# Moving the key and query transposes of a fused attention and double-FFN kernel: where they are issued, when their split copies run, and two small edits beside them

## The chip, the core and the metric

The kernel runs on one core of a Trainium2 chip. The metric is the device time of one execution in microseconds (us), the lower the better. One execution before the change was recorded by the hardware profiler; its trace is what all rows below are read from. The engines are named as the profile names them: PE (TensorE, the matrix engine; PEld is its weight load), DVE (VectorE), ACT (ScalarE), POOL (GpSimd), SP (SyncE, which here issues DMAs).

## The reference

What is computed is a local-and-global attention over 2 batches, 8 heads, 768 positions and 64 dimensions a head, and two dense feed-forward layers (FFN) on its result:

```python
# attention: 8 global keys, a causal window of 96 keys
scores = scale * q @ k.T + bias          # bias = -slope[h] * distance
scores = where(is_global | is_local, scores, -1e9)
a = exp(scores - scores.max(-1)); a = a / (a.sum(-1) + 1e-9)
x = (a @ v) rearranged to (1536 tokens, 512)
# FFN 1
h = x @ w_in1;  g = max(h, 0) + log1p(exp(-|h|));  x = g @ w_out1
# FFN 2
h = x @ w_in2;  g = h / (1 + exp(-1.702 * h));     out = g @ w_out2
```

All inputs and outputs are fp32. w_in has shape 512 x 2048 and w_out 2048 x 512 in both layers.

## The kernel before

Every product that needs fp32 precision is made of three matmuls on a high and a low part of each operand (`kh`, `kl`, `qh`, `ql` for keys and queries, `gh`, `gl` in the FFN). ACT makes the high part as a rounding copy, and DVE makes the low part as the difference to it; so `kl` always comes after its `kh`, and `ql` after its `qh`.

The attention runs over 12 blocks n of 128 queries. Each block has two halves g of four heads, which gives 24 halves s = 2n + g. One trip of the loop `for s in range(ns + 3)` issues work of several halves, in the order in which it is written (the scheduler is switched off there, and every engine takes its instructions in that order):

- on PE: `turn_r` (L540, tile `qps`, the reciprocal sums spread over a tile, odd trips only), `turn(s-1)` (L608, tile `t`, transposes of the exponentials), `scores(s+1)` (L571, tiles `s`), `turn_q` or `turn_k` (both through `turned`, L489, tile `qps`: four transposes of a block's queries or keys), `values(s-2)` (L630, tile `o`);
- on ACT: `split_q` (L504, `qh`) or `split_k` (L516, `kh`), `weights_of(s)` (L596, four exponentials with their sums, tile `pr`), in odd trips one operation of the weight converter that `tick` releases (L145, tile `t`, or L155, tile `w`) and `copy_r` (L545, `y`), then `copy_p(s-1)` (L615, or L617 for a narrow half, tile `pt`), which brings the transposed exponentials from PSUM to SBUF;
- on DVE: pieces of the weight converter (L143 to L160), the low part `ql` (L506) or `kl` (L518), `reduce(s+1)` (L584: bias added, minimum taken, tiles `pr` and `mins`), and in even trips `weigh` (L531, L532) and `normalise` (L553 to L555, tiles `y`, `x0h`, `x0l`).

"Even" and "odd" below mean the parity of s in its trip. Three buffers matter. The PSUM tile `t` of `turn` exists once (`ps_t`, one buffer of two banks), so that `turn(s)` can't begin before `copy_p(s-1)` has read it. The `qps` tiles alternate between the PSUM banks `h2` and `h3` of `h_pool`, in the order in which they are asked for; `turn_k`, `turn_r` and `turn_q` share them. The first FFN unit, `first(0)` (L254, tile `h`), takes `h2` too, and is issued in trips 20 to 22. A block that begins a batch has 128 keys only, one that doesn't has 256, called narrow and wide here.

`check_counts` (L95 to L99) does five tiny DVE operations on the two scalars n_global and n_local. At the end of the kernel `staged` copies the last four accumulators of FFN 2 from PSUM to SBUF, one for each 128 rows of the result; the last of them is cut in two column halves, the first copied by DVE (L322) and the second by ACT (L323). `drain` sends each of the four out by one DMA (L365), the last from ACT's queue.

Of the kernel before, what the change touches and what calls it, by code (L numbers as in the profile page):

```python
# [8 lines left out]
F32 = mybir.dt.float32  # L9
# [4 lines left out]
AF = mybir.ActivationFunctionType  # L14
# [3 lines left out]
P = 128  # L18
# [7 lines left out]
TB = 512  # L26
# [9 lines left out]
def attention_two_ffns(ctx: ExitStack, tc: tile.TileContext, q, k, v, n_global, n_local,  # L36
# [10 lines left out]
    nc = tc.nc  # L47
# [16 lines left out]
    conv = ctx.enter_context(tc.tile_pool(name="conv", bufs=3))  # L64
# [29 lines left out]
    def check_counts():  # L94
        nc.vector.tensor_scalar(flag[:, 0:1], NL, 1.0, None, op0=ALU.is_lt)  # L95
        nc.vector.tensor_scalar(flag[:, 1:2], NL, float(WIN), None, op0=ALU.is_gt)
        nc.vector.tensor_tensor(flag[:, 0:1], flag[:, 0:1], flag[:, 1:2], op=ALU.max)
        nc.vector.tensor_scalar(flag[:, 1:2], NG, float(GLB), None, op0=ALU.is_gt)
        nc.vector.tensor_tensor(flag[:, 0:1], flag[:, 0:1], flag[:, 1:2], op=ALU.max)  # L99
# [128 lines left out]
    def ffn_phase(x1, slots, work, h_pool, weights, converter):  # L228
# [8 lines left out]
        acc, gs, st, part, pools = {}, {}, {}, {}, {}  # L237
# [77 lines left out]
        def staged(t, l, last=False):  # L315

            for m in range(4):
                if m % 2 == 0:
                    both = conv.tile([P, 2, TB], F32, tag="t", name="o")
                o = both[:, m % 2, :]  # L320
                if last and m == 3:
                    nc.vector.tensor_copy(o[:, :TB // 2], acc[l, t][m][:, :TB // 2])  # L322
                    nc.scalar.activation(o[:, TB // 2:], acc[l, t][m][:, TB // 2:], AF.Copy)  # L323
                elif m % 2:
                    nc.vector.tensor_copy(o, acc[l, t][m])
                else:
                    nc.scalar.activation(o, acc[l, t][m], AF.Copy)  # L327
                yield m, o, both
# [20 lines left out]
        def drain(l, t):  # L349
            if l == 0:  # L350
                xh, xl = x_tiles(f"y{t}")
                xs[1, t] = (xh, xl)
                sums = acc[l, t]
                if t in part:
                    sums = part[t]
                    for m in range(4):
                        nc.vector.tensor_tensor(sums[m], sums[m], acc[l, t][m], op=ALU.add)
                for m in range(4):
                    nc.scalar.activation(xh[:, m, :], sums[m], AF.Copy)
                    e = nc.gpsimd if t in part else nc.vector  # L360
                    e.tensor_tensor(xl[:, m, :], sums[m], xh[:, m, :].bitcast(F32), op=ALU.subtract)
            else:
                for m, o, _ in staged(t, 1, t == 0):
                    q = nc.scalar if t == 0 and m == 3 else nc.sync
                    q.dma_start(out[t * TB + m * P:t * TB + (m + 1) * P, :], o)  # L365

        def rest(u0, parts, acc_pool):
            pools.update(parts=parts, acc=acc_pool)
# [22 lines left out]
    def split_attention(actx, x1, h_pool, converter, first, bend, budget=1600):  # L391
# [100 lines left out]
        def own(i):  # L492

            return WIN + GLB + i % RING * BLK


        def turn_q(n):
            qts[n] = turned(raw[n]["qn"], n == 1)
# [10 lines left out]
        def turn_k(n):  # L509
            raw[n]["kn"] = turned(raw[n]["kn"], n == 1)  # L510
# [49 lines left out]
        def scores(s):  # L560
            n, g = halves[s]
            i = blocks[n][1]
            w, at = (NW, own(i) - WIN - GLB) if i else (P, own(0))
            qh, ql = qts[n]
            banks = [h_pool.tile([P, TB], F32, tag=f"h{e}", name=f"s{e}") for e in range(2)]
            ps[s] = ([x.rearrange("p (j k) -> p j k", j=2) for x in banks], w)
            for j in range(2):
                for m, (a, c) in enumerate(((qh, kh), (qh, kl), (ql, kh))):
                    for e in range(2):
                        es = slice(e * D, (e + 1) * D)  # L570
                        nc.tensor.matmul(ps[s][0][e][:, j, :w], lhsT=a[es, 2 * g + j, :],  # L571
                                         rhs=c[es, 2 * g + j, at:at + w], start=m == 0, stop=m == 2)

        def reduce(s):

            n, g = halves[s]
            banks, w = ps.pop(s)
            pr = pr_pool.tile([P, 2, 2, NW], F32, tag="pr", name="pr")
            table = bias_w if w == NW else bias_0
            prs[s] = (pr, w)  # L580
            for j in range(2):
                for e in range(2):
                    h = 4 * g + 2 * j + e
                    nc.vector.tensor_tensor_reduce(pr[:, j, e, :w], banks[e][:, j, :w], table[:, h, :], 1.0, 3.0e38,  # L584
                                                   op0=ALU.add, op1=ALU.min,
                                                   accum_out=mins[:, H * n + h:H * n + h + 1])
# [13 lines left out]
        def turn(s):  # L600
            pr, w = prs[s]
            nch = w // P
            t = ps_t.tile([P, 2 * TB], F32, tag="t", name="t")
            t = t.rearrange("p (j c e k) -> p j c e k", j=2, c=2, e=2)
            for j in range(2):
                for c in range(nch):
                    for e in range(2):
                        nc.tensor.transpose(t[:, j, c, e, :], pr[:, j, e, c * P:(c + 1) * P], ident)  # L608
            pts[s] = (t, nch)

        def copy_p(s):
            t, nch = pts[s]
            pt = p_pool.tile([P, 2, 2, 2, P], F32, tag="pt", name="pt")
            if nch == 2:
                nc.scalar.activation(pt, t, AF.Copy)  # L615
            else:
                nc.scalar.activation(pt[:, :, 0], t[:, :, 0], AF.Copy)  # L617
            pts[s] = pt
            prs.pop(s)
# [13 lines left out]
        def run(*parts):  # L633
            for part in parts:
                for _ in part or ():
                    pass

        ns = len(halves)
        nb = len(blocks)
# [21 lines left out]
        load(3)  # L661
        yield
        scores(0)
        reduce(0)
        turn_q(1)
        for s in range(ns + 3):
            n, g = divmod(s, 2)
            live = n < nb
            if g == 1 and 0 < n < nb - 3:
                load(n + 3)  # L670
            if g == 0 and 0 < n < nb:
                load_v(n)

            if g == 1 and 0 <= n - 1 < nb:
                turn_r(n - 1)
            if s >= 1 and s - 1 < ns:
                turn(s - 1)
            if s + 1 < ns:
                scores(s + 1)
            if s == 0:  # L680
                spin(5)
            if s == 1:
                turn_q(2)

            kept = iter(())
            if g == 0 and n + 1 < nb:
                kept = split_k(n + 1)
            if g == 1 and 1 < n + 1 < nb - 1:
                kept = split_q(n + 2)
            if s != 2:  # L690
                next(kept, None)
            if live:
                weights_of(s)
            if s == 1:
                copy_p(0)
            converter.tick()
            if s == 0:
                window_masks()
                bias(bias_w, dw, 0)
            if g == 0 and 0 <= n - 1 < nb:  # L700
                weigh(n - 1)
            if s > 1 and g == 0:
                converter.pump(budget // 2)
            run(kept)
            if s > 1 and g == 1:
                converter.pump(budget // 2)
            if s + 1 < ns:
                reduce(s + 1)
            if s == 0:
                bias(bias_w, dw, 4)  # L710
            if s < 2:
                run(split_q(s + 1))
            if s == 4:
                check_counts()
            if g == 0 and 0 <= n - 2 < nb:
                normalise(n - 2)
            if s > 1:
                converter.pump(budget // 2 * (s == 2 or g) if s + 1 < ns else budget)
            if g == 1 and 0 <= n - 1 < nb:
                copy_r(n - 1)  # L720
            if 1 < s <= ns:
                copy_p(s - 1)
            if g == 0 and 0 < n < nb - 2:
                turn_q(n + 2)
            if g == 1 and n + 2 < nb:
                turn_k(n + 2)
            if s >= 2 and s - 2 < ns:
                values(s - 2)

            if ns - 4 <= s < ns - 1:  # L730
                first(0, ((0,), (1,), (2, 3))[s - ns + 4])
            if ns - 1 <= s < ns + 2:
                bend(s - ns + 1)
                if s < ns + 1:
                    first(s - ns + 2)
            yield
# [173 lines left out]
```

## Time and profile before

| quantity | value |
|---|---|
| median of 3 runs | 642.05 us (641.81 to 642.26) |
| the profiled execution, its own time | 641.64 us |
| its span in the trace | 639.8 us |
| granted TensorE clock, mean | 0.999 of full speed |
| PE busy | 624.7 us (98%) |
| DVE busy | 397.5 us (62%) |
| ACT busy | 368.9 us (58%) |
| POOL busy | 20.6 us (3%) |
| chain that ended last | PE 90%, DVE 7%, DMA 1%, issue 1% |

The span is what the trace shows from its first instruction to its last; the execution's own time lies 1.8 us above it. Busy shares are means over the whole span, in which the attention (to about 118 us, mixed with the first FFN units from about 95 us) and the FFN (to about 633 us) differ much from each other.

### The profile page before, as it was taken

Reading aid. Unit: us, or ns where it says so; the run is one execution under the profiler, and the core shown is the slowest. Engines: PE = TensorE matmul, PEld = TensorE weight load, DVE = VectorE, ACT = ScalarE, POOL = GpSimd, SP = SyncE. Lnnn points to the kernel's source line nnn. Section 1 sums busy time; section 2 is a strip of 40 time slices with the busy share of each in tenths; the row PEclk is TensorE's granted clock in tenths of the full one; section 3 lists DMA queues with packets and bytes.
Section 4 is the critical chain, followed back from the end, with each engine's and each line's share of the span. In section 5 each row is a group of like instructions: output and inputs, shape, how many; then the busy total and the mean of one; then the engine's idle time right before and its main releaser. Section 6 shows DMA issues by size and latency. Waiting matters only on the chain.

```text
span 639.8 us, 9005 instructions
## 1 busy us (share of the span) xinstructions
PE 624.7 (98%) x3443; PEld 515.0 (80%) x3443; DVE 397.5 (62%) x757; ACT 368.9 (58%) x683; POOL 20.6 (3%) x46
## 2 busy tenths in 40 slices
PE   8899999999999999999999999999999999999995
PEld 7687778887888888888888888888888888888884
DVE  6999999799999757999469996751121111211111
ACT  6999998778787667887567863532232222222221
POOL 3200100000000000000000022000000000000000
PEclk9999999999999999999999999999999999999999
DMA  9967846931000003520015670000010000100001
GB/s 213 255 165 168 191 135 218 345 127 59 8 2 0 1 0 132 197 67 1 0 66 188 211 237 24 0 1 1 0 67 0 2 0 1 66 1 1 0 1 71
DMA packets 65715, 51.52 MB, mean 81 GB/s; under 512 B 41920, under 2 KB 58304, under 8 KB 65664
## 3 DMA queue, kind: packets, MB, share of 16 engines
q1 hardware_dynamic: 65232, 50.60, 27.1%
q8 instruction: 29, 0.48, 0.3%
q10 hardware_dynamic: 432, 0.26, 0.1%
q14 instruction: 22, 0.18, 0.1%
HBM read 44.70 MB, written 4.19 MB: 76 GB/s over the span
## 4 chain that ended last, share of the span: by engine, by line
PE 90%; DVE 7%; DMA 1%; issue 1%; SPq 0%; POOL 0%; ACT 0%; DVEq 0%; POOLq 0%
PE h L254 41%; PE acc L306 21%; PE acc L308 20%; DVE pr L584 2%; PE o L630 2%; PE t L608 2%; PE s L571 1%; PE qps L540 1%; PE qps L489 1%; DMA raw<-in_moe_w_out 1%; PE spin L419 1%; DVE t L153 1%; DVE kl L518 1%; DVE y L553 0%; DVE ql L506 0%
## 5 line engine op out<-in xcount | busy, mean ns | idle before, releaser
L275 DVE TENSOR_TENSOR gl<-g,gh 128x512 fp32r<-128x512 f32 x96 | 67.2, 700 | 173.4 <-ACT gh L273 173.2
L306 PE MATMUL acc<-gh,w 128*128 128x512 f32 x384 | 126.4, 390 | 0.0
L308 PE MATMUL acc<-w,gh 128*128 128x512 f32 x384 | 125.6, 389 | 0.0
L273 ACT ACTIVATE gh<-g 128x512 fp32r<-128x512 f32 x96 | 60.4, 629 | 88.3 <-PE acc L308 81.5
L306 PEld LDWEIGHTS acc<-gh,w 128*128 128x128 f32 x384 | 72.1, 188 | 15.2 <-ACT o L327 0.4
L308 PEld LDWEIGHTS acc<-w,gh 128*128 128x128 f32 x384 | 72.1, 188 | 15.1
L281 ACT ACTIVATE g<-h 128x512 f32<-128x512 f32 x48 | 28.7, 598 | 91.8 <-PE h L254 85.5
L306 PE MATMUL acc<-gl,w 128*128 128x512 f32 x192 | 75.1, 391 | 0.0
L308 PE MATMUL acc<-w,gl 128*128 128x512 f32 x192 | 74.7, 389 | 0.0
L284 ACT ACTIVATE e<-h 128x512 f32<-128x512 f32 x48 | 28.5, 593 | 39.4 <-PE h L254 37.1
L262 DVE SCALAR_TENSOR_TENSOR g<-c,g 128x512 f32<-128x512 f32 x48 | 32.9, 686 | 25.2 <-ACT g L288 25.1
L596 ACT ACTIVATE pr<-pr,mins 128x256 f32<-128x256 f32 (+1 forms) x96 | 45.8, 483 | 2.4 <-DVE mins L584 2.2
L254 PE MATMUL h<-x0h,w 128*128 128x512 f32 x128 | 43.2, 396 | 0.1
L306 PEld LDWEIGHTS acc<-gl,w 128*128 128x128 f32 x192 | 36.0, 188 | 8.7 <-DVE gl L275 1.3
L155 ACT ACTIVATE w<-t 128x1024 fp32r<-128x1024 f32 x32 | 33.8, 1058 | 15.1 <-DVE t L153 12.2
L254 PE MATMUL h<-y0h,w 128*128 128x512 f32 x128 | 42.0, 389 | 0.0
L254 PE MATMUL h<-y2h,w 128*128 128x512 f32 x128 | 42.0, 389 | 0.0
L254 PE MATMUL h<-x1h,w 128*128 128x512 f32 x128 | 42.0, 389 | 0.0
L254 PE MATMUL h<-y1h,w 128*128 128x512 f32 x128 | 42.0, 389 | 0.0
L254 PE MATMUL h<-x2h,w 128*128 128x512 f32 x128 | 42.0, 389 | 0.0
L308 PEld LDWEIGHTS acc<-w,gl 128*128 128x128 f32 x192 | 36.0, 188 | 7.4
L153 DVE SCALAR_TENSOR_TENSOR t<-raw,t 128x1024 int32<-128x1024 int32 x32 | 39.9, 1247 | 2.3 <-ACT t L145 2.3
(134 smaller groups left out, 1128.8 us busy)
## 6 DMA issues: line engine op xcount, KB each, us to landing
raw<-in_moe_w_in SPq DMA_DIRECT2D x32, 512.0 KB, 4.6
raw<-in_moe_w_out SPq DMA_DIRECT2D x32, 512.0 KB, 5.6
kn<-in_k SPq DMA_DIRECT2D x12, 256.0 KB, 4.4
qn<-in_q SPq DMA_DIRECT2D x12, 256.0 KB, 4.9
vn<-in_v SPq DMA_DIRECT2D x12, 256.0 KB, 3.5
out<-o SPq DMA_DIRECT2D x11, 256.0 KB, 2.1
vp<-vn SPq DMA_DIRECT2D x10, 192.0 KB, 3.9
part<-o SPq DMA_DIRECT2D x2, 512.0 KB, 3.8
```

The costliest lines, as they stand in the source:

```text
L153: nc.vector.scalar_tensor_tensor(t, top, -2 ** 31, t, op0=ALU.bitwise_and, op1=ALU.bitwise_or)
L155: s["later"](lambda: nc.scalar.activation(w[:, 0, :], t.bitcast(F32), AF.Copy))
L254: nc.tensor.matmul(h, lhsT=w[:, a, c * P:(c + 1) * P], rhs=b[:, c, :], start=c == 0 and n == 0, stop=c == KD - 1 and n == 2)
L262: nc.vector.scalar_tensor_tensor(st[u - 1]["g"], st[u - 1]["c"], -1.0, st[u - 1]["g"], op0=ALU.add, op1=ALU.subtract)
L273: nc.scalar.activation(gh, g, AF.Copy)
L275: nc.vector.tensor_tensor(gl, g, gh.bitcast(F32), op=ALU.subtract)
L281: nc.scalar.activation(g, s["h"], AF.Gelu_apprx_sigmoid)
L284: nc.scalar.activation(e, s["h"], AF.Abs)
L306: nc.tensor.matmul(o, lhsT=wo[:, a, ms], rhs=g, **kw)
L308: nc.tensor.matmul(o, lhsT=g[:, ms], rhs=wo[:, a, :], **kw)
L584: nc.vector.tensor_tensor_reduce(pr[:, j, e, :w], banks[e][:, j, :w], table[:, h, :], 1.0, 3.0e38, op0=ALU.add, op1=ALU.min, accum_out=min ...
L596: nc.scalar.activation(pr[:, j, e, :w], pr[:, j, e, :w], AF.Exp, bias=mins[:, H * n + h:H * n + h + 1], scale=-1.0, accum_out=sums[n][:, h ...
```

## The change

It has four parts.

1. `turn_k` and `turn_q` move from the end of a trip to right behind `turn(s-1)` of a later trip, ahead of `scores(s+1)`. `turn_k(n+1)` is now issued in the even trip of block n (before: at the end of the odd trip ahead of it), and `turn_q(n+2)` in the odd trip of block n (before: in the even trip ahead of it).
2. The split is cut in two places of a trip: the high part (`kh`, `qh`, ACT) now stands behind the exponentials of `weights_of(s)`, and the low part (`kl`, `ql`, DVE) behind the minima of `reduce(s+1)`. Before, both stood ahead of these.
3. `check_counts` moves from trip 4 to ahead of `reduce(0)`, before the loop.
4. The last 128 rows, which DVE and ACT copy in halves, get a buffer for each half, and go out by two DMAs of half the columns (one from SP, one from ACT) in place of one from ACT.

```diff
                 if last and m == 3:
+                    other = conv.tile([P, TB], F32, tag="t", name="o")
                     nc.vector.tensor_copy(o[:, :TB // 2], acc[l, t][m][:, :TB // 2])
-                    nc.scalar.activation(o[:, TB // 2:], acc[l, t][m][:, TB // 2:], AF.Copy)
+                    nc.scalar.activation(other[:, TB // 2:], acc[l, t][m][:, TB // 2:], AF.Copy)
+                    o = o, other
...
-                    q = nc.scalar if t == 0 and m == 3 else nc.sync
-                    q.dma_start(out[t * TB + m * P:t * TB + (m + 1) * P, :], o)
+                    rows = slice(t * TB + m * P, t * TB + (m + 1) * P)
+                    if isinstance(o, tuple):
+                        for q, part_of, c in zip((nc.sync, nc.scalar), o, (slice(0, TB // 2), slice(TB // 2, TB))):
+                            q.dma_start(out[rows, c], part_of[:, c])
+                    else:
+                        nc.sync.dma_start(out[rows, :], o)
...
         scores(0)
+        check_counts()
         reduce(0)
...
                 turn(s - 1)
+            if g == 0 and 2 <= n + 1 < nb:
+                turn_k(n + 1)
+            if g == 1 and 3 <= n + 2 < nb:
+                turn_q(n + 2)
             if s + 1 < ns:
                 scores(s + 1)
...
-            if g == 1 and 1 < n + 1 < nb - 1:
+            if g == 1 and 3 <= n + 2 < nb:
                 kept = split_q(n + 2)
-            if s != 2:
-                next(kept, None)
+            if s == 0:
+                next(kept)
             if live:
                 weights_of(s)
             if s == 1:
                 copy_p(0)
+            if s > 0:
+                next(kept, None)
             converter.tick()
...
-            run(kept)
+            if s == 0:
+                run(kept)
             if s > 1 and g == 1:
                 converter.pump(budget // 2)
             if s + 1 < ns:
                 reduce(s + 1)
+            run(kept)
...
-            if s == 4:
-                check_counts()
...
-            if g == 0 and 0 < n < nb - 2:
-                turn_q(n + 2)
-            if g == 1 and n + 2 < nb:
-                turn_k(n + 2)
```

In the changed file every line from `staged`'s new tile on stands 2 to 6 lines further down: L489 becomes L495, L504 L510, L540 L546, L571 L577, L584 L590, L608 L614, L615 L621, L630 L636.

PE's order, two trips in a row early in the loop, trip 3 (odd) and then trip 4 (even). Here `t` is the transposed exponentials, `qps` with `qn` or `kn` the turned queries or keys, `qps` with `sum` is `turn_r`, and the 12 matmuls of each `scores` (tiles `s`) are left out at the dots. Before:

```order
L540 MATMUL qps<-ident,sum 64x128 x8
L608 MATMUL t<-ident,pr 128x128 x8
...
L489 MATMUL qps<-ident,kn 128x128 x4
L630 MATMUL o<-pt,vn 64x128 x4
L608 MATMUL t<-ident,pr 128x128 x8
...
L489 MATMUL qps<-ident,qn 128x128 x4
```

After:

```order
L546 MATMUL qps<-ident,sum 64x128 x8
L614 MATMUL t<-ident,pr 128x128 x8
L495 MATMUL qps<-ident,qn 128x128 x4
...
L636 MATMUL o<-pt,vn 64x128 x4
L614 MATMUL t<-ident,pr 128x128 x8
L495 MATMUL qps<-ident,kn 128x128 x4
```

The queries are now turned in the odd trip and the keys in the even one, and each stands between the transposes `t` and the scores.

ACT's order from the exponentials of trip 4 to the end of trip 5 and the start of trip 6. Before:

```order
L596 ACTIVATE pr,sum<-pr,mins 128x256 x4
L615 ACTIVATE pt<-t 128x1024
L504 ACTIVATE qh<-qps 128x512
L596 ACTIVATE pr,sum<-pr,mins 128x256 x4
L155 ACTIVATE w_0_493<-t 128x1024
L545 ACTIVATE y<-qps 128x512
L615 ACTIVATE pt<-t 128x1024
L516 ACTIVATE kh<-qps 128x4x128
```

After:

```order
L602 ACTIVATE pr,sum<-pr,mins 128x256 x4
L522 ACTIVATE kh<-qps 128x4x128
L621 ACTIVATE pt<-t 128x1024
L602 ACTIVATE pr,sum<-pr,mins 128x256 x4
L510 ACTIVATE qh<-qps 128x512
L155 ACTIVATE w_0_498<-t 128x1024
L551 ACTIVATE y<-qps 128x512
L621 ACTIVATE pt<-t 128x1024
```

In the odd trip `qh` has moved from ahead of the exponentials to behind them, and `w`, `y` and `pt` of the same trip still follow it.

DVE's order around the low part of the keys and the minima of trip 6 (the second pair of `pr,mins` rows of each `reduce` left out at the dots). Before:

```order
L518 TENSOR_TENSOR kl<-qps,kh 128x4x128
L584 ISA pr,mins<-s_614,bias_w 128x256
L584 ISA mins 128x1
L584 ISA pr,mins<-s_615,bias_w 128x256
```

After:

```order
L590 ISA pr,mins<-s_614,bias_w 128x256
...
L590 ISA mins 128x1
L524 TENSOR_TENSOR kl<-qps,kh 128x4x128
L559 TENSOR_TENSOR y<-o,y 128x512
```

The low part now stands behind all four minima, and `normalise` behind it.

## Rows read from the trace of the kernel before

**Rows 1.** Busy time by engine (us, instructions), granted clock, DMA: a late attention stretch; FFN.

```profile
75.00:87.50 12.50, 11.76 (x147) 9.66 (x146) 12.36 (x39) 12.25 (x35) 0.99 (x2) 1.00 0.83 211
95.00:633.00 538.00, 537.98 (x2489) 443.22 (x2487) 310.65 (x468) 282.12 (x443) 7.07 (x4) 1.00 0.18 60
```

**Rows 2.** What PE waited for, 8 to 120 us: total us, times, longest us.

```profile
PE qps L489 <- DVE ql L506: 4.0, 5, 1.4
PE qps L540 <- DVE kl L518: 1.4, 2, 1.0
```

**Rows 3.** Timeline of PE, 79 to 95 us: start, us, engine, line, tiles.

```profile
84.03 0.39 PE L571 MATMUL s<-kh,qh 64*128 64x256 f32 x2
...
86.45 1.04 PE L540 MATMUL qps<-ident,sum 128*64 128x128 f32 x16
87.42 1.09 PE L608 MATMUL t<-ident,pr 128*128 128x128 f32 x8
88.44 0.39 PE L571 MATMUL s<-kh,qh 64*128 64x256 f32 x2
...
92.42 0.38 PE L571 MATMUL s<-kh,qh 64*128 64x256 f32 x2
...
94.54 0.50 PE L254 MATMUL h<-x0h,w 128*128 128x512 f32 x1
```

**Rows 4.** Timeline of PE, 13.5 to 26.5 us; in brackets idle before, and releaser.

```profile
14.22 0.66 PE L489 MATMUL qps<-ident,qn 128*128 128x128 f32 x4
...
23.94 1.09 PE L608 MATMUL t<-ident,pr 128*128 128x128 f32 x8 [0.68 <-ACT pt L615]
24.96 0.39 PE L571 MATMUL s<-kh,qh 64*128 64x256 f32 x2
```

**Rows 5.** Timeline of ACT, 13.5 to 26.5 us.

```profile
14.98 0.60 ACT L504 ACTIVATE qh<-qps 128x512 fp32r<-128x512 f32 x1 [0.66 <-PE qps L489]
15.47 0.50 ACT L596 ACTIVATE pr<-pr,mins 128x256 f32<-128x256 f32 x1
...
21.36 1.14 ACT L145 ACTIVATE t<-t,ebias 128x1024 int32<-128x1024 int32 x1
22.41 0.57 ACT L545 ACTIVATE y<-qps 128x512 f32<-128x512 f32 x1
22.88 1.00 ACT L615 ACTIVATE pt<-t 128x1024 f32<-128x1024 f32 x1
```

**Rows 6.** Timeline of ACT, 79 to 95 us.

```profile
79.93 1.04 ACT L155 ACTIVATE w<-t 128x1024 fp32r<-128x1024 f32 x1
80.88 0.57 ACT L545 ACTIVATE y<-qps 128x512 f32<-128x512 f32 x1
```

**Rows 7.** Timeline of DVE, 79 to 96 us.

```profile
93.81 0.68 DVE L518 TENSOR_TENSOR kl<-qps,kh 128x512 fp32r<-128x512 f32 x1
94.41 0.41 DVE L584 CUSTOM_DVE_ANT_0 pr<-s,bias_w 128x256 f32<-128x256 f32 x1
...
95.78 0.68 DVE L553 TENSOR_TENSOR y<-o,y 128x512 f32<-128x512 f32 x1
```

**Rows 8.** Timelines of DVE, 8 to 10, 17 to 26.5 and 27.5 to 31 us.

```profile
9.41 0.29 DVE L584 CUSTOM_DVE_ANT_0 pr<-s,bias 128x128 f32<-128x128 f32 x1 [0.87 <-PE s L571]
...
18.33 0.68 DVE L518 TENSOR_TENSOR kl<-qps,kh 128x512 fp32r<-128x512 f32 x1
...
28.88 0.15 DVE L95 TENSOR_SCALAR flag<-nval 128x1 f32<-128x1 f32 x1
...
29.58 0.68 DVE L553 TENSOR_TENSOR y<-o,y 128x512 f32<-128x512 f32 x1
```

**Rows 9.** Timeline of all engines, 632 to 640 us, the last two lines.

```profile
633.68 0.38 ACT L323 ACTIVATE o<-acc 128x256 f32<-128x256 f32 x1 [0.54 <-DVE o L322]
634.09 0.36 ACTq L365 DMA_DIRECT2D out<-o  x1
```

## The prediction

> **What bounds the kernel now.** I read the busy time by windows first. In a late stretch of the attention DVE is busy 12.36 of 12.50 us, ACT 12.25 and PE 11.76, while from 95 to 633 us PE is busy 537.98 of 538.00 us, at a granted clock of 1.00 in both [rows 1]. So the FFN takes its time whatever the change does, since none of its matmuls is touched, and what counts is when its first matmul `h` can start (94.54 us, [rows 3]): a delay there goes through to the end. Then I read what PE waits for in the attention. The largest items are the two that this change is about: the turned queries or keys wait for the low part `ql` (4.0 us in 5 waits) and the reciprocal sums for `kl` (1.4 us in 2), because they share the banks `h2` and `h3` [rows 2]. But DVE is the fullest engine in that stretch, so PE's waits for it are mostly slack. The timeline of PE gives the pace: the scores of half 19 start at 84.03 and those of half 21 at 92.42 [rows 3], so a block takes 8.39 us; from half 5 (24.96, [rows 4]) to half 21 it is 67.46 us for eight blocks.
>
> **The change, part by part.**
>
> *Turning and splitting.* No instruction of the attention is added or removed: the same transposes, copies and subtractions stand elsewhere in each engine's order. What matters is therefore which chains between the in-order queues close into a loop. ACT in an odd trip now issues exponentials, `qh`, a held converter operation, `y`, `pt`. Before, `qh` read queries that PE had turned a trip earlier. Now it reads those that PE turns in the same trip, behind `turn_r` and `t`, and three more ACT operations stand behind `qh`, the last of which is the `pt` that frees the only buffer of `t` for the next trip's transposes. This closes a loop from PE to ACT and back once a block, which did not exist before. Its length, from the scores of one odd half to those of the next, each step from one start to the next start:
>
> - scores, values and four turning transposes of PE: 84.03 to 86.45 (they stand there in a row) = 2.42 us [rows 3]. (In the changed loop the scores and values come at its start and the four transposes of the keys at its end, just ahead of the next scores; the sum is the same.)
> - `turn_r`: 86.45 to 87.42 = 0.97; `t`: 87.42 to 88.44 = 1.02 [rows 3].
> - from the start of the turning of the queries to the start of `qh` on an ACT that waits for it: 14.22 to 14.98 = 0.76 [rows 4, 5].
> - `qh` 14.98 to 15.47 = 0.49 [rows 5].
> - the held operation: L155 79.93 to 80.88 = 0.95 [rows 6], or L145 21.36 to 22.41 = 1.05 [rows 5]; the two take turns, one in each odd trip.
> - `y` 22.41 to 22.88 = 0.47 [rows 5].
> - `pt` and its hand-over to PE: 22.88 to 23.94, where `t` is seen to wait for it = 1.06 [rows 4, 5].
> - the next trip's `t`: 1.02 again [rows 3].
>
> The sum is 2.42 + 0.97 + 1.02 + 0.76 + 0.49 + 0.95 + 0.47 + 1.06 + 1.02 = 9.16 us, and 9.26 with L145. A loop is a floor: whatever the other engines do, a block can't be shorter than this. It is 0.77 to 0.87 us longer than the 8.39 us of now. ACT's own work of a block, some 8.2 us by its busy share (12.25 of 12.50 x 8.39), and DVE's, some 8.3, both fit into 9.2, so neither makes it longer still.
>
> Eight blocks lie between halves 5 and 21, four with each held operation: 4 x 9.16 + 4 x 9.26 = 73.68. One of these blocks begins a batch and is narrow: scores (0.9), `t` and `pt` (1.02 and 1.06) of its halves are half as wide, which I estimate at 1.4 us less in its loop, and 0.35 us less in the next, which has its values. That leaves 71.93, against 67.46: **+4.5 us**.
>
> The loop is entered late too. `turn_q(3)` of trip 3 takes the bank that `kl(2)` must have been read from, and `kl(2)` now stands behind the minima. These then start where `kl` did, at 18.33 [rows 8]; four minima take 94.41 to 95.78 = 1.37 and `kl` 0.68 [rows 7], so `kl` ends at 20.38. From there 0.04 to PE, then 0.76 + 0.49 + 1.05 + 0.47 + 1.06 + 1.02 + 0.59 (the share of a turning in the 2.42, estimated from its rows' 0.60 to 0.66 us) give scores of half 5 at 25.86 in place of 24.96: **+0.9 us**.
>
> Last, `first(0)` takes bank `h2`, which holds the last keys until `kl(11)` has read them. Before, `kl` came first (93.81, 0.68 long, [rows 7]) and `h` started 0.05 us behind it, 2.12 us after the scores of half 21 began [rows 3]. Now scores (1.01, estimated as 92.42 to the end of their last matmul), minima 1.37, `kl` 0.68 and 0.05 follow each other: 3.11 us, **+1.0 us**. Nothing else covers this: what PE could do in the meantime is issued behind `h`.
>
> What does the change gain in the same place? PE's 5.4 us of waits for `ql` and `kl` [rows 2] go, but PE was not what set the pace of 8.39 us, and now waits for `pt` instead. So I take nothing off.
>
> *The counts.* Five tiny operations, from 28.88 to 29.58 us, cost DVE 0.70 us where it is full; they move to where it waits 0.87 us for the first scores (9.41) [rows 8]. With DVE as the bound this would be worth 0.70. With the loop above as the bound, DVE has slack, and it is worth 0. I take 0; ends -0.70 and 0 (they fit into the wait, so no loss).
>
> *The tail.* ACT's half of the last rows starts 0.04 us behind DVE's end (0.54 idle, released by DVE) and the DMA is issued at 634.09 [rows 9]. With a buffer of its own the ACT half could start as early as DVE's. But the changed program's ACT copy still carries a wait on the same count of DVE's work, so I let it start where it did. DVE's half may leave about 0.45 us earlier, ACT's leaves as before and is half as large. Ends: -0.45 (both halves go early) and +0.36 (a second DMA is one more issue, of the length of the row of the first [rows 9], and lands late); I take **-0.1 us**, since the later of the two halves sets the end and leaves at the old time.
>
> The sum is 4.5 + 0.9 + 1.0 - 0.1 = +6.3 us: 641.64 + 6.3 = 647.9. The profiled execution lies 0.41 us below the median of the runs, which is within their spread, so I forecast **647.9 us**.
>
> The Trainium skill (Perfetto Trace Analysis, section Identifying the Most-Contended Engine) says that a kernel generally gains by work on the engine with the highest occupancy, for DVE and ACT by the busy share. By that rule alone DVE, the fullest in rows 1, would set the attention's time after the change too, and the sum would be that of the first rival below. I go by the loop, because it is made of starts that the trace shows and does not ask which engine is fullest.
>
> **The rivals.**
>
> *DVE stays the bound (no change).* If ACT were not kept by `qh` in the odd trip, DVE would go on at 8.39 us a block, the counts would give back 0.70, and `h` would wait for a `kl` that ends 1.37 later [rows 7]: -0.70 + 1.37 - 0.1 = +0.6, 642.2 us. For it speaks DVE's 12.36 of 12.50 us; against it, that the order of ACT puts `pt` behind `qh`, and that an in-order engine can't pass a waiting instruction. It decides if the loop's sum is under 8.39, so if 0.8 of my nine steps is hidden.
>
> *PE's removed waits count (faster).* If the waits of rows 2 are what keeps DVE from its last per cent, DVE's idle share (0.14 of 12.50 us, over 67 us 0.75) goes as well, with the 0.70 of the counts and the 0.45 of the tail: -1.9, 639.7 us. It needs the loop under about 8.3 us, and a `kl(11)` that is early enough for `h`, which means DVE 1.4 us ahead of now at the end of the attention. Nothing in the rows puts it there.
>
> *The loop is entered and left worse than I count (slower still).* In this loop ACT's high parts, DVE's low parts and POOL's copies of keys into the ring each come one trip later, closer to the scores that read them. If one of them is 0.4 us late in each block, eight blocks make 3.2 us more: 651 us. Against it: `kl` ends about 3.1 us behind the start of an odd half's scores by the steps above, and the scores that need it start about 4.4 us behind (2.42 + 0.97 + 1.02), so 1.3 us is left.
>
> **How the numbers follow.** My forecast with its bounds 0.80; no change 0.09; faster 0.05; slower still 0.06. Its own bounds: 0.4 us a block less than I sum (if hand-overs overlap) makes 3.2 us less, 644.7; some 0.3 a block more makes 650.3. The range 644.5 to 650.5 holds these and leaves the three rivals out, 0.20 together. A measurement of this kernel tells 0.2% (1.28 us) from no change: faster 0.05; same 0.08 (most of the first rival); slower 0.87 (the forecast, the third rival, and the rest of the first).
>
> **What would show it.** In the profile after: ACT idle ahead of `qh` (L510), released by the turning of the queries (L495), about 0.8 us in each odd trip; PE idle ahead of `t` (L614), released by ACT's `pt` (L621), about once a block; odd scores some 9.2 us apart; the first `h` at about 101 us, released by `kl`; DVE's busy share in the attention down to about 0.9; PE from there on without gaps, as before. PE's waits for `ql` and `kl` ahead of `qps` should be all but gone, and the last DMA issued at the old distance from the last matmul. If odd scores stay 8.4 us apart, the loop is wrong and the first rival is right; if they are apart by more than 9.5, something else is late, and the waits of PE's scores would name it.

## The result, and the profile after

The changed kernel takes 647.96 us (median of 4 runs, 646.5 to 649.79) against 641.93 us before (641.65 to 642.26): a ratio of 1.0088, 95% interval 1.0069 to 1.0107. It is slower by 6.0 us, close to the 647.9 us of the forecast. Measured once more with 6 runs it has a median of 648.37 us (646.0 to 650.03; ratio 1.0091, interval 1.0066 to 1.0115). The kernel before spreads less around its median (641.36 to 644.57 in the 17 runs beside this second measurement). This spread has its own cause, told below; the profiled execution here took 649.79 us, and one of the second measurement 646.16 us.

The two windows that answer to [rows 1], of the changed kernel (us; busy time of PE, PEld, DVE, ACT and POOL with instructions; granted clock, DMA share, GB/s):

```profile
75.00:87.50 12.50, 10.81 (x132) 9.11 (x130) 12.29 (x37) 11.70 (x33) 3.07 (x8) 1.00 0.79 177
104.00:641.00 537.00, 536.96 (x2485) 442.73 (x2482) 308.61 (x460) 280.46 (x436) 7.09 (x4) 1.00 0.18 60
```

The FFN is as full as before: PE waits 0.04 us in 537. What was lost was lost before its first matmul. In the attention PE's busy time falls from 11.76 to 10.81 us. DVE hardly shows it in this stretch (12.29 for 12.36), probably because a converter that is fed by trips puts different amounts of work in different stretches; from 50 to 62.5 us DVE was busy 12.21 before and 11.40 after.

What PE waits for from 8 to 130 us in the changed kernel, the answer to [rows 2]:

```profile
PE t L614 <- ACT pt L621: 10.3, 8, 1.7
PE h L254 <- DVE kl L524: 1.2, 1, 1.2
...
PE s L577 <- DVE ql L512: 0.3, 1, 0.3
```

The waits of the turned tiles that the profile put down to `ql` and `kl` are gone, 5.4 us of them. In their place stand eight waits of the transposes `t` for ACT's `pt`, 10.3 us, and one of the first `h` for `kl`. That is the predicted exchange, with a small remainder: in some odd trips the turned queries still start just behind the end of `kl`, as told below.

Here is one trip round the loop on PE, and the end of the attention (timeline of PE, start, us; in brackets idle before, and releaser):

```profile
38.88 0.39 PE L577 MATMUL s<-kh,qh 64*128 64x256 f32 x2
...
40.70 1.04 PE L546 MATMUL qps<-ident,sum 128*64 128x128 f32 x16
41.68 1.09 PE L614 MATMUL t<-ident,pr 128*128 128x128 f32 x8
42.60 0.60 PE L495 MATMUL qps<-ident,qn 128*128 128x128 f32 x4
...
46.33 1.09 PE L614 MATMUL t<-ident,pr 128*128 128x128 f32 x8 [1.19 <-ACT pt L621]
47.26 0.60 PE L495 MATMUL qps<-ident,kn 128*128 128x128 f32 x4
47.79 0.39 PE L577 MATMUL s<-kh,qh 64*128 64x256 f32 x2
...
99.64 0.39 PE L577 MATMUL s<-kh,qh 64*128 64x256 f32 x2
...
102.88 0.47 PE L254 MATMUL h<-x0h,w 128*128 128x512 f32 x1 [1.22 <-DVE kl L524]
```

And ACT's part of the same trip:

```profile
43.24 0.60 ACT L510 ACTIVATE qh<-qps 128x512 fp32r<-128x512 f32 x1 [0.56 <-PE qps L495]
43.74 1.14 ACT L145 ACTIVATE t<-t,ebias 128x1024 int32<-128x1024 int32 x1
44.78 0.59 ACT L551 ACTIVATE y<-qps 128x512 f32<-128x512 f32 x1
45.25 1.02 ACT L621 ACTIVATE pt<-t 128x1024 f32<-128x1024 f32 x1
```

Read them as one chain. PE turns the queries at 42.60, ACT waits for them and starts `qh` at 43.24, then the held operation, `y` and `pt` follow without a gap, PE waits 1.19 us for `pt`, and from `t` at 46.33 the next odd scores follow at 47.79. From 38.88 that is 8.91 us, and no step of it shows slack. The odd scores of the other wide blocks stand 8.7 to 9.0 us apart, in this execution and in the one of 646.16 us.

### The profile page after: what moved, and what is told of

Read it like the earlier page. It is cut to its first block, busy times and chain, and to the rows that moved or that the text cites. A ratio compares the mean times of both kernels' runs of the same rounds, so it can differ in the third digit from the quotient of the medians.

```text
span 648.4 us, 9007 instructions
## 1 busy us (share of the span) xinstructions
PE 625.7 (96%) x3443; PEld 518.0 (80%) x3443; DVE 398.3 (61%) x757; ACT 370.0 (57%) x683; POOL 21.2 (3%) x46
## 4 chain that ended last, share of the span: by engine, by line
PE 93%; ACT 4%; DVE 1%; DMA 1%; issue 1%; DVEq 0%; ACTq 0%
PE h L254 40%; PE acc L306 20%; PE acc L308 20%; PE t L614 4%; PE s L577 2%; PE o L636 2%; PE qps L546 2%; PE qps L495 2%; ACT pt L621 1%; ACT t L145 1%; DMA ints<-in_n_local 1%; ACT y L551 1%; ACT w L155 1%; ACT qh L510 0%; PE spin L425 0%
## 5 line engine op out<-in xcount | busy, mean ns | idle before, releaser
L155 ACT ACTIVATE w<-t 128x1024 fp32r<-128x1024 f32 x32 | 33.8, 1058 | 15.7 <-DVE t L153 12.8
```

The costliest lines, as they stand in the source:

```text
L155: s["later"](lambda: nc.scalar.activation(w[:, 0, :], t.bitcast(F32), AF.Copy))
```

## The experiments

**The changed kernel measured again.**

> The changed kernel unchanged, for its spread. The loop theory explains a fixed part: about 2.3 us from the pace of the blocks, 1.1 at the first h and -0.1 at the end, so 3.3 us, and a late entry of about 1 us: 646.0 to 646.5 us whenever TensorE's clock is granted in full. The clock theory says that all above that is a stretch at half clock in the first 25 us, so runs with a lower mean clock (0.99) lie up to 3.5 us higher and runs with 0.997 or more lie at 646. If runs at a full clock lie above 647, the loop theory has the entry wrong.

It gave 648.37 us; its profiled execution 646.16 us, at a granted clock of 1.00 in every stretch of the attention. There half 5 starts at 25.96 (before 24.96), half 21 at 95.67, `h` at 98.90. So the blocks from half 5 to half 21 take 69.71 us (before 67.46), `h` comes 3.23 us behind half 21 (before 2.12), and the rest differs by 0.16 us: 1.00 + 2.25 + 1.11 + 0.16 = 4.5 us, all of 646.16 - 641.64. This is what the order costs at a full clock; 646.16 lies within the expected 646.0 to 646.5.

**The counts alone.**

```diff
         scores(0)
+        check_counts()
         reduce(0)
...
-            if s == 4:
-                check_counts()
```

> The kernel before with the check of the counts moved ahead of the first minima and nothing else. Loop theory: DVE is the bound in the attention of this kernel, so 0.70 us of work less there: 641.2 to 641.6 us. Clock theory, with the counts as the cause of the half-clock stretch: some runs 2 to 3.5 us above 642 with a clock below 0.997. If neither, within 0.2 us of before.

641.18 us against 641.92, ratio 0.9984 (0.9971 to 0.9997): the 0.7 us that DVE saves where it is the bound. `h` starts at 94.08 for 94.54. One of its 12 runs lay above 642 us (643.55), so the early check isn't what spreads the runs of the changed kernel.

**Does `pt` stand in a loop, or is ACT only fuller?** Two kernels add the same work to ACT, a second copy `y` in each odd trip. In the first it stands ahead of `pt`, as the cut below shows, in the second behind it.

```diff
             nc.scalar.activation(y, rts[n], AF.Copy)
+            if n < nb - 2:
+                nc.scalar.activation(y, rts[n], AF.Copy)
```

> The changed kernel with the ACT copy y done twice in each odd trip, both ahead of the copy of the transposed exponentials (0.47 us more work of ACT a block). Loop theory: the second copy is a term of the loop, so wide blocks go from 8.9 to 9.4 us and the eight blocks between halves 5 and 21 take 3.8 us more: 649.5 to 650.5 us without a half-clock stretch. Rival (the loop has slack): no more than 1 us.

> The same second copy, but placed behind the copy of the transposed exponentials: the same work on ACT, outside the loop. Loop theory: ACT's own work of a block is some 8.8 us then, still under 8.9, so the blocks stay at 8.9 to 9.0 us and the time within 1 us of the changed kernel (646 to 647 without a half-clock stretch). Rival (ACT's total work sets the pace, not the loop): the same 3.8 us more as in the run with the copy ahead.

Ahead of `pt`: 654.89 us (ratio 1.0207, 1.0184 to 1.0231), which is more than expected, with a mean granted clock of 0.987 to 0.994 in its four runs. Behind it: 647.33 us (1.0072, 1.0051 to 1.0094; clock 0.994 to 0.997), no more than the changed kernel. Two odd scores in a row of the first, on PE's timeline:

```profile
93.08 0.39 PE L579 MATMUL s<-kh,qh 64*128 64x256 f32 x2
...
102.63 0.39 PE L579 MATMUL s<-kh,qh 64*128 64x256 f32 x2
```

ACT ahead of them, in the same kernel:

```profile
89.43 0.59 ACT L551 ACTIVATE y<-qps 128x512 f32<-128x512 f32 x1
90.05 0.60 ACT L553 ACTIVATE y<-qps 128x512 f32<-128x512 f32 x1
90.55 1.02 ACT L623 ACTIVATE pt<-t 128x1024 f32<-128x1024 f32 x1
```

And the same two odd scores of the second:

```profile
88.08 0.39 PE L579 MATMUL s<-kh,qh 64*128 64x256 f32 x2
...
96.98 0.39 PE L579 MATMUL s<-kh,qh 64*128 64x256 f32 x2
```

Ahead of `pt` this block takes 9.55 us, behind it 8.90. From the first `y` to `pt` are 1.12 us for 0.47, so 0.65 more: in this block the whole addition between `qh` and `pt` is added to the block. (I had expected 0.47; the second copy onto the same tile starts only when the first has ended.) Five of the eight blocks from half 5 to half 21 grow by 0.62 to 0.65 us against the changed kernel at full clock. Two grow by 0.4 only (they had been held up a little by `kl`, see below), and the first by 1.23, with the clock at 0.50 in part of it. The eight take 74.94 us, 5.23 more than the changed kernel. The second kernel takes 69.98 us. This settles that the loop sets the pace, and ACT's total work doesn't.

**The held operation out of the loop.** The operation that `tick` releases is put behind `pt` in odd trips.

```diff
+            held = []
+            if g == 1 and s > 1 and live:
+                held, converter.hold = converter.hold, held
             converter.tick()
...
                 copy_p(s - 1)
+            for what in held:
+                what()
```

> The changed kernel with the held converter operation of each odd trip (L145 or L155 on ACT) moved behind the copy of the transposed exponentials of that trip; PE and DVE keep the changed order. Loop theory: this operation of 0.95 or 1.04 us is a term of the loop, so the loop falls from 8.9 to about 7.9 us and DVE's 8.4 us a block is the bound again: odd scores 8.4 apart, 2.0 to 2.3 us less than the changed kernel, 643.7 to 644.3 us where no half-clock stretch comes in. Rival (the pace is set by something that does not run through these ACT operations, such as the low parts behind the minima): odd scores stay 8.9 apart, 646 us or more.

645.67 us (ratio 1.0049, 1.0037 to 1.0061), and 644.17 in the profiled execution, 2.0 less than the changed kernel at full clock, as expected in sum but not in its parts. Half 5 starts at 24.62, 1.34 earlier, and the eight blocks take 68.73 us, only 0.98 less; `h` comes 3.82 us behind half 21. The first four blocks from half 5 alternate between 9.6 and 8.1 us, as those of the kernel before do (9.8 and 8.0 at its start), and PE still waits 5.5 us for `pt`. The loop is shorter, not open, and a second chain shows. In the three longest blocks (9.62, 9.59 and 9.29 us) the turned queries start 0.10 or 0.11 us behind the end of a `kl`, 0.6 to 1.0 us later than behind `t` alone; the profile puts these waits down to `t`. So the low part in the shared bank, late behind the minima, holds PE up as soon as ACT's loop is shorter.

**Only the last low part put back.**

```diff
+            if n + 1 == nb - 1:
+                run(kept)
             if s + 1 < ns:
                 reduce(s + 1)
             run(kept)
```

> The changed kernel with the low part of the last keys alone put back ahead of the minima. The first h then waits for it as in the kernel before: 2.1 us behind the scores of half 21 in place of 3.2, and 1.1 us less than the changed kernel: 645.0 us without a half-clock stretch. If the wait is hidden by later work, no difference (646.1).

644.96 us (ratio 1.0036, 1.0023 to 1.0049). In its profile half 21 starts at 96.92 and `h` at 98.85, 1.93 us behind: this wait is a term of its own, 1.1 to 1.3 us, and isn't hidden.

**Other ways to open the loop, which failed.** Three kernels each alter one part of the changed order.

Queries split behind `pt`, on the changed kernel (both `next(kept)` and `run(kept)` of odd trips follow `copy_p`):

> The changed kernel with the split of the queries (high and low part) moved behind the copy of the transposed exponentials in its trip; PE's order stays as changed. Loop theory: the copy no longer waits for the queries of its own trip, so the loop is open: blocks of 8.4 us, 642.3 to 643.2 us. Rival (PE's order, turning between the transposes and the scores, is the cost): no better than the changed kernel, 646 us or more.

Only the keys moved, the queries turned and split as before:

> The changed kernel with the queries put back (turned a trip earlier, split ahead of the exponentials and of the minima), the keys left as changed. Loop theory: the loop runs through the queries alone, so the blocks go back to 8.4 us; the first h still waits for the last keys behind the minima (+1.1); 642.3 to 643.2 us. Rival (any early turning behind the transposes costs the same, or the low parts behind the minima do): half or more of the loss stays, 644.5 us or more.

The queries turned ahead of `t` in odd trips:

> The changed kernel with one swap on PE: in odd trips the queries are turned ahead of the transposes of the exponentials. Loop theory: qh can start up to 0.9 us earlier, but the queries then wait for the last keys' low part in their bank (about 3.1 us behind the odd scores), so the loop falls by some 0.65 to about 8.25 us, under DVE's 8.4: 644 to 645 us. Rival (the bank shared with the low part of the keys is what counts): PE waits for kl ahead of the queries, the blocks stay at 8.9 us or grow, 646 us or more.

They gave 646.76, 652.05 and 648.30 us, none as the loop theory had them; each came out where the rival beside it stood. What DVE and ACT wait for from 8 to 130 us with the queries split behind `pt` (total us, times, longest):

```profile
DVE ql L512 <- ACT qh L510: 1.7, 3, 0.9
```

```profile
ACT pr L602 <- DVE mins L590: 4.1, 8, 1.2
```

What PE waits for where only the keys are moved:

```profile
PE qps L546 <- DVE kl L524: 11.4, 8, 2.5
```

And what PE waits for where the queries are turned ahead of `t`:

```profile
PE qps L495 <- issue: 9.1, 8, 1.9
PE t L614 <- ACT pt L621: 3.3, 8, 0.8
```

There, one of the eight waits of the queries, and on DVE the `kl` that shares their bank:

```profile
50.49 0.63 PE L495 MATMUL qps<-ident,qn 128*128 128x128 f32 x4 [1.89 <-issue]
```

```profile
49.70 0.69 DVE L524 TENSOR_TENSOR kl<-qps,kh 128x512 fp32r<-128x512 f32 x1
```

In the first DVE now waits for a later `qh`, its minima come later, and ACT's exponentials wait 4.1 us for them (1.8 in the changed kernel); besides, in six of nine odd trips the queries start 0.09 or 0.10 us behind the end of `kl`. As I read it, one loop is opened and others bind, so this kernel doesn't tell the two theories apart. In the second the `qps` tiles are asked for in the order keys, queries, sums, so `turn_r` now takes the bank that the keys were in, and waits for a `kl` that stands behind the minima, eight times. (The clock is a part of its time too: 0.989 to 0.991 in all five runs.) The changed order (keys, sums, queries) gives that bank to the queries, which come later. In the third, PE's wait ahead of the queries has grown to 9.1 us. The profile names no releaser, but all eight waits end 0.09 to 0.11 us behind the end of `kl` in the shared bank, as in the two lines (49.70 + 0.69 = 50.39, then 50.49). The wait for `pt` falls from 10.3 to 3.3 us, for nothing.

**The split cut without the turning moved.** On the kernel before, high parts behind the exponentials and low parts behind the minima, and nothing else.

```diff
-            if s != 2:
-                next(kept, None)
+            if s == 0:
+                next(kept)
...
+            if s > 0:
+                next(kept, None)
             converter.tick()
...
-            run(kept)
...
                 reduce(s + 1)
+            run(kept)
```

> The kernel before with only the split cut as in the changed kernel (high parts behind the exponentials, low parts behind the minima); the turning stays where it was. If the low parts behind the minima cost by themselves, through the bank that turn_r shares with the keys, this is slower than before by 4 us or more (646 to 652), with PE's turn_r waiting for kl in each block. If the loop through the turning of the same trip is the only cost, the blocks stay at 8.4 us and only the first h is later: 642.5 to 643.5 us.

673.39 us, a ratio of 1.0469 (1.0451 to 1.0487), far more than expected. PE's waits:

```profile
PE qps L489 <- issue: 19.3, 9, 2.3
PE qps L540 <- DVE kl L518: 6.4, 7, 2.4
PE h L254 <- DVE kl L518: 1.2, 1, 1.2
```

With the turning where it was, the late split alone costs 31 us. The second line shows `turn_r` waiting for a `kl` that now stands behind the minima. The first names no releaser, but all its nine waits are of turned keys, and end 0.09 or 0.10 us behind the end of a `ql`, which stands there too. Part of the 31 us is the clock: the five runs have a mean of 0.976 to 0.988, and the profiled one, the slowest, 0.87 from 8 to 127 us. Moving the turning to where the bank is free takes back most of the 31 us, and costs the loop. The reverse, the turning moved and the split left early, was not run, so what that half costs by itself isn't shown.

**A kernel that beats both.** The counts early, and the last 128 rows copied by DVE alone:

```diff
                 if last and m == 3:
-                    nc.vector.tensor_copy(o[:, :TB // 2], acc[l, t][m][:, :TB // 2])
-                    nc.scalar.activation(o[:, TB // 2:], acc[l, t][m][:, TB // 2:], AF.Copy)
+                    nc.vector.tensor_copy(o, acc[l, t][m])
```

> The kernel before with the early check of the counts, and the last 128 rows copied by DVE alone in one piece (0.69 us) in place of DVE's half and then ACT's half (0.42 + 0.04 + 0.38). The copy then ends some 0.15 us earlier, and so does the end; with the counts 641.0 to 641.3 us. Each is under what a measurement tells, the trace has to show it.

640.85 us against 642.18: ratio 0.9980 (0.9971 to 0.9988), 1.3 us faster than the kernel before, and some 7 us faster than the changed one, which was measured apart from it. Its last copy and DMA:

```profile
632.42 0.69 DVE L322 COPY o<-acc 128x512 f32<-128x512 f32 x1 [0.67 <-PE acc L308]
633.14 0.36 ACTq L364 DMA_DIRECT2D out<-o  x1
```

The DMA is issued 0.72 us behind the start of DVE's copy; before it was 0.87 (633.22 to 634.09). With the 0.7 us of the counts that is 0.85 of the 1.3 us; the rest is within the interval (0.8 to 1.9 us).

## Why the prediction was right, and where it was not

**The bound and the mechanism** held: the FFN passed the delay on, PE's waits for `ql` and `kl` all but went and bought nothing, and the loop through `qh`, the held operation, `y` and `pt` set the pace. The two copies of `y` show it.

**The term of the eight blocks was mis-sized.** I summed 9.16 us a loop with L155 and 9.26 with L145, and +4.5 us for eight; in the profile after, a loop with L155 measured 9.02 and one with L145 8.91, and the eight +2.25. The steps that I took too long: from `t` to the turning behind it I used the distance from `t` to scores (1.02), it takes 0.92 and 0.93, and stands in the loop twice; from the turning to `qh` I used the one early row (0.76), it takes 0.64; and the turning itself took 0.53 for 0.59. That is 0.37 us of the loop. The bound of 0.4 us a block in the range covers this. I also let the loops differ by the 0.1 us of their held operations alone. One wide loop with L155 does take 8.82 us, 0.09 less than with L145. But in three of the eight blocks `kl` ends so late that the turned queries start 0.10 us behind it, and so 0.1 to 0.2 us later than `t` would let them. The loop of 9.02 us is one of these, in the profile after:

```profile
50.91 0.69 DVE L524 TENSOR_TENSOR kl<-qps,kh 128x512 fp32r<-128x512 f32 x1
```

```profile
50.60 1.09 PE L614 MATMUL t<-ident,pr 128*128 128x128 f32 x8
51.69 0.63 PE L495 MATMUL qps<-ident,qn 128*128 128x128 f32 x4
```

Here the queries follow `t` by 1.09 us in place of 0.92. My sum had no term for this.

**The entry** was right: half 5 at 25.96, predicted 25.86. The queries of trip 3 do wait for `kl(2)`, although the profile names `t`; in the execution of 646.16 us:

```profile
19.88 0.70 DVE L524 TENSOR_TENSOR kl<-qps,kh 128x512 fp32r<-128x512 f32 x1
```

```profile
20.68 0.63 PE L495 MATMUL qps<-ident,qn 128*128 128x128 f32 x4 [0.86 <-PE t L614]
```

**The first `h`** was right too: 3.23 us behind half 21, predicted 3.11.

**The counts** were worth 0.7 us where DVE is the bound. That they are worth nothing in the changed kernel fits its sum, but no run takes them out of it.

**The tail** was right in its reason. In the changed kernel, the answer to [rows 9]:

```profile
641.96 0.38 ACT L324 ACTIVATE o<-acc 128x256 f32<-128x256 f32 x1 [0.54 <-DVE o L323]
642.05 0.40 SPq L369 DMA_DIRECT2D out<-o  x1
642.38 0.36 ACTq L369 DMA_DIRECT2D out<-o  x1
```

ACT's half still waits for DVE's, with a buffer of its own. From the start of DVE's copy to the end of the execution are 8.29 us here and 8.42 before. But the other profiled executions give 8.28 to 8.80 with the new tail and 8.15 to 8.45 with the old, so a gain of 0.1 us isn't shown. What both halves share is the PSUM bank that they read. The Trainium skill (PSUM — Partial Sum Buffer, section PSUM bank collisions raise a hardware error) says that two engines must be kept from the same bank and quadrant at the same time, reads with reads too; that the wait stays when the buffers are apart agrees with it.

**What the sum left out** is the clock. The order costs 4.5 us at a full clock, but the median lies 6.0 to 6.5 above before. The missing 1.5 to 2 us come from executions in which TensorE's clock falls. In the ten runs of the changed kernel the time goes with the mean granted clock: 646.0 to 646.5 us at 0.997 and 0.998, 647.4 at 0.996, 648.3 to 648.5 at 0.992 and 0.993, 649.8 and 650.0 at 0.990. Here are the first `t` in the loop and the stretch from 25 to 27 us in the execution of 646.16 us:

```profile
24.50 1.09 PE L614 MATMUL t<-ident,pr 128*128 128x128 f32 x8 [1.69 <-ACT pt L621]
```

```profile
25.00:27.00 2.00, 2.00 (x24) 1.70 (x24) 1.93 (x3) 2.00 (x8) 0.00 (x0) 1.00 1.08 238
```

In the kernel with only the last `kl` put back, which has the same order up to there, the same two read:

```profile
24.27 1.92 PE L614 MATMUL t<-ident,pr 128*128 128x128 f32 x8 [1.69 <-ACT pt L621]
```

```profile
25.00:27.00 2.00, 2.00 (x12) 1.67 (x10) 1.93 (x3) 1.17 (x6) 0.00 (x0) 0.50 1.06 245
```

And the stretch in the kernel with the second `y` behind `pt`:

```profile
25.00:27.00 2.00, 2.00 (x11) 1.67 (x9) 1.93 (x3) 1.72 (x8) 0.00 (x0) 0.50 0.96 226
```

At 1.00 (2.4 GHz) the eight transposes take 1.09 us, at 0.50 (1.2 GHz) 1.92, and in the 2 us from 25 to 27 PE does 24 instructions or only 11 or 12 (not all of the same kind). In both kernels the fall comes right behind a wait of 1.69 us for the first `pt` in the loop. Half 5 then starts 1.0 us later than in the execution at full clock (26.98 and 27.00), and the next odd scores lose 0.2 more. The same wait was 0.68 us before [rows 4], and no clock fell behind it there. The execution of 649.79 us had lost its clock already at about 11 us, until about 21, and ahead of everything that the turning moves; one window out of it:

```profile
15.00:17.50 2.50, 2.35 (x17) 2.02 (x16) 0.00 (x0) 0.60 (x1) 1.17 (x3) 0.50 1.02 343
```

So that the forecast of 647.9 hit the median is luck: an overlong loop (2.2 us too much) and a clock that wasn't in the sum (about 2 too little) cancel. At full clock the changed kernel takes 646 us, still in the range.

**The rivals.** The first (DVE stays the bound, 642.2) was wrong, and with it the rule on the most contended engine that stood beside it: the Trainium skill (Perfetto Trace Analysis, section Identifying the Most-Contended Engine) says generally, and this kernel, whose engines were all above nine tenths, is paced by a chain across three of them. The second failed for the same reason. The third, that something comes late besides the loop, is seen in a small way only: `kl` is late in three of eight blocks, by 0.1 to 0.2 us, and late for the bank of the turned queries, not for the scores.

**Left open:** how many executions lose their clock at 11 us and how many later, and why the changed kernel's lose it more often than those of before (a mean clock of 0.994 or less in 6 of its 10 runs, and in 4 of the 17 runs before beside the second measurement).

## What to carry to other kernels

Before an instruction is moved in an engine's in-order queue, write down what stands behind it there and who waits for that, and sum each closed chain over one period: its length is a floor under the pace, however much slack every engine shows. A place where PSUM banks alternate is part of such a chain, since the order of requests decides who waits for whose reader. Work that moves to a place where its engine idles was free here (the counts), and removing waits of an engine that didn't set the pace bought nothing. A wait whose releaser the profile doesn't name, or names doubtfully, can be settled by setting its end beside the end of the last read of the same bank.

## What was not expected of the hardware

Two ACT copies onto the same tile start 0.62 us apart (89.43 and 90.05), where `y` and a following copy of another tile start 0.47 apart (44.78 and 45.25).

An idle stretch of 1.69 us on PE was followed by 0.50 of the full clock, from about 24.4 to 27.8 us, in two profiled kernels, and by 1.00 in an execution of the changed kernel with the same wait at the same place.
